# Two Fourier-and-GLU layers on one core: the first quad's row sums as f32 products with scaled diagonals, and a new order for the opening

## The chip, the cores and the metric

The kernel runs on one core of one Trainium2 chip. The core has TensorE (PE) for matmuls, whose results land in the eight banks of PSUM, VectorE (DVE), ScalarE (ACT), GpSimd (POOL) and SyncE (SP), which here issues most DMAs. Each engine works through its own queue in order. The time is that of one execution of the program on the chip, in microseconds; a kernel's figure is the median of its runs.

## The reference

Two rounds of the same two layers on `x` (2048 rows of 640), all in f32:

```python
x = x + _A_ref(_layernorm(x), dft_seq_re, dft_seq_im, dft_hid_re, dft_hid_im)
x = x + _B_ref(_layernorm(x), w_gate, w_up, w_down)
# _A_ref: a = x @ hid_re.T; b = x @ hid_im.T; y = seq_re @ a - seq_im @ b
# _B_ref: h = sigmoid(x @ w_gate) * (x @ w_up); y = h @ w_down     (F = 1728)
```

## The kernel before

**Folding.** The Fourier matrices are symmetric, so the kernel adds and subtracts mirrored rows and columns first and multiplies by a quarter of the matrix. The 2048 rows stand in four *quads* (i = 0 to 3) of four *groups* of 128 rows each, A, B, C and D (GA to GD). Within a row, column c and column 640 - c are added (the even half e, 321 columns) and subtracted (the odd half o, 320 columns): `fold_columns`, in the opening's list `cg i g` for one group and `col i k` for two. The rows of B and C are needed in reverse order: they are loaded as they lie, multiplied by a reversed identity on PE in f32 (`turn`, into a pair of PSUM banks called a twin), and brought back to SBUF by ACT (`turned`).

**Scale and join.** LayerNorm gives every row a factor; the statistics come from `stats`, `square` and `means`, the factor from `power` (ACT) and `scale` (DVE), into `quads[i]`, column 19, and the constants from the means into `coef[i]`. Then `re` and `ro` (ACT, L783 and L785) scale the even and odd halves of B and D, `dd` (DVE, L788; `de` and `do`, L792, for quad 1) adds scaled A and C to them, and `join` (DVE, L829) forms A + C and A - C. So every quad ends as two e parts and two o parts.

**High and low halves.** Everything that PE multiplies in the dense work is f16 in two parts. `jhi` (ACT, L839) rounds to f16, `jlo` (DVE, L845, and a small copy on ACT, L849) writes what is left. `chi` and `clo` do so for the sequence matrix, `whhi` and `whlo` for the hidden one, `wshi` and `wslo` for the gate and up weights (all L269 on ACT and L271 on DVE).

**Products.** `seq i tp` (PE, L980) multiplies quad i by its part of the sequence matrix, tp = 0 for the even and 1 for the odd rows; quads 0 and 1 sum into one set of banks and 2 and 3 into another. `evhi` and `ev` bring these sums out as high and low f16. `hid q ph` (PE, L1065) multiplies by the hidden matrix; `hidev`, `first`, `im`, `sums`, `difs` and `add` bring the result into x. The second LayerNorm of the first rows (`nst`, `cen`, `nvar`, `npow`, `nscale`, `nhi`, `nlo`), transposes (`tp`, `tph`, `tpl`) and the first gate and up products (`gu`, L1343) end the opening. After it the program runs the rest of the two rounds from a planner's list with due times; the change leaves that list alone.

**Order.** The opening's order is written out by hand in one string, `OPENING`. Its steps are emitted one after the other, and each goes to the end of its engine's queue, so the string fixes the order on every engine. `junk n` is n f16 matmuls of zeros (L376) with no reader. The loads of x, of the sequence matrix and of the first weights are issued by SP ahead of all of it (`wld` loads later weights). Before, PSUM is divided in the opening into two twins (two banks each) and four single banks; after the last `turned` the twins' four banks become single ones (`drop_twins`).

SBUF is one tensor, `big`, from which `take` hands out slots; their addresses come from a search over the times at which they are taken and dropped.

Of the kernel before, what the change touches and what calls it, by code (L numbers as in the profile page):

```python
# [138 lines left out]
class Slot:  # L139
# [37 lines left out]
    first 1, first 0, hid 0 1, wslo 0 1, ev 1 1 1, ev 1 1 0, wslo 1 0, evhi 1 1 2, im, sums, hid 1 0, hidev 1 0,  # L177
    hid 1 1, hid 2 0, add 0, nst 0, hidev 1 1, cen 0, wshi 0 0, difs, add 1, hidev 2 0, nst 1, nvar 0, wslo 0 0,
    cen 1, npow 0, nscale 0, ev 1 1 2, nst 2, nst 3, nhi 0, nhi 1, cen 3, nvar 1, nlo 0, nlo 1, npow 1, mid, hid 2 1,
    tp 0, tp 1, tph 0, wld 4 0, wld 3 1, wld 4 1, wld 3 0, tpl 0, tpl 1, nscale 1, tph 1, cen 2, nhi 3, midhi, gu 0 0,  # L180
# [1976 lines left out]
```

## Time and profile before

| | |
|---|---|
| runs | 1142.88, 1141.91, 1138.86 us; median 1141.91 |
| profiled execution | 1141.29 us, of which the span 1139.5 |
| mean granted TensorE clock | 0.994 |
| PE busy | 1110.4 us, 97% of the span, 9030 matmuls |
| DVE, ACT, POOL busy | 761.8, 538.5, 348.8 us |
| first `seq` product, first `hid` product, first `gu` product | 40.20, 67.55, 85.77 us |

In a row of the timeline the start (us) comes first, then the length, the engine, the line of the kernel, the operation, what it writes and reads, the shape, and xN where N instructions were merged; in brackets is the idle time of the engine before it and what ended that. In a row of groups the busy time and the mean of one instruction in ns stand behind the bar. In a row by stretch the busy time of PE, PEld (weight loads), DVE, ACT and POOL follow the length, then the granted clock (1.00 is full), the DMA engines' share and GB/s. In a row of waits stand the total in us, how often, and the longest.

### The profile page before, as it was taken

The page shows a single profiled execution, that of the slowest core. Times are in us where ns is not written, and L with a number is a line of the kernel's source. Part 1 is how long each engine was busy: PE and PEld are TensorE (multiplying, and loading weights), DVE is VectorE, ACT ScalarE, POOL GpSimd, SP SyncE. Part 2 cuts the span into 40 slices and gives each one's busy share as a digit, 9 for nine tenths or more (in the row PEclk, how much of TensorE's full clock was granted, in tenths as well). Part 3 has the DMA queues.
Part 4 walks back from the last instruction along what each step waited for, and adds up shares of the span by engine and source line. Part 5 has one row for each costly group of instructions (what it writes and reads, how often), then busy time and mean ns, then how long its engine had stood idle before and what let it go on. Part 6 is the DMA issues. An engine that isn't in the chain of part 4 may idle for free. (4 is left out here: it accounts for less than half of the span.)

```text
span 1139.5 us, 23456 instructions
## 1 busy us (share of the span) xinstructions
PE 1110.4 (97%) x9030; PEld 883.1 (78%) x9030; DVE 761.8 (67%) x1678; ACT 538.5 (47%) x1187; POOL 348.8 (31%) x568
## 2 busy tenths in 40 slices
PE   5799999999999999999999999999999999999997
PEld 3668446788878887788878888778887888788875
DVE  6994998766656877485667877834674668426751
ACT  6975583355534653255525544314541555225430
POOL 1001564432445353431350203031553322132001
PEclk9989999999999999999999999999999999999999
DMA  8434685877595756968521662474957973799411
GB/s 247 151 125 156 240 312 157 246 244 221 164 238 193 243 181 174 244 212 302 193 108 43 186 222 94 125 240 164 265 168 150 322 238 104 100 238 292 157 41 39
DMA packets 154447, 214.72 MB, mean 188 GB/s; under 512 B 74655, under 2 KB 99505, under 8 KB 154326
## 3 DMA queue, kind: packets, MB, share of 16 engines
q1 hardware_dynamic: 135622, 165.04, 48.7%
q0 software_dynamic: 18560, 47.93, 14.1%
q8 instruction: 72, 1.18, 0.4%
q14 instruction: 49, 0.40, 0.1%
q10 hardware_dynamic: 144, 0.16, 0.0%
HBM read 173.04 MB, written 25.44 MB: 174 GB/s over the span
## 5 line engine op out<-in xcount | busy, mean ns | idle before, releaser
L1390 PE MATMUL acc<-big 128*128 128x256 f16 x4698 | 516.6, 273 | 1.8 <-ACT big L1394 1.4
L1390 PEld LDWEIGHTS <-big 128*128 128x128 f16 x4698 | 459.6, 98 | 56.4 <-issue 1.5
L1547 PE MATMUL acc<-big 128*128 128x320 f16 x2624 | 357.7, 299 | 0.0
L1547 PEld LDWEIGHTS <-big 128*128 128x128 f16 x2624 | 256.7, 98 | 99.5
L1608 POOL DMA_DIRECT2D big<-in_ct x256 | 174.3, 686 | 269.2 <-DVE big L1617 145.2
L1394 ACT ACTIVATE big<-acc 128x256 f32<-128x256 f32 x348 | 130.3, 382 | 233.2 <-PE acc L1390 229.6
L1458 DVE TENSOR_TENSOR big<-big 128x512 f16<-128x512 f32 x87 | 59.9, 689 | 112.3 <-ACT big L1457 112.3
L1580 ACT ACTIVATE big<-big 128x768 f32<-128x768 f32 (+10 forms) x110 | 81.3, 739 | 89.4 <-DVE big L1617 72.7
L1343 PE MATMUL acc<-big 128*128 128x256 f16 (+1 forms) x705 | 114.6, 325 | 0.5 <-ACT big L673 0.5
L1343 PEld LDWEIGHTS <-big 128*128 128x128 f16 x705 | 68.9, 98 | 45.0 <-issue 0.7
L1436 ACT ACTIVATE big<-big 128x512 f32<-128x512 f32 x87 | 53.4, 628 | 53.6 <-DVE big L1427 53.2
L271 DVE SCALAR_TENSOR_TENSOR big<-big 128x640 f16<-128x640 f32 (+7 forms) x82 | 62.9, 799 | 7.3 <-ACT big L269 7.2
L1446 DVE SCALAR_TENSOR_TENSOR big<-acc,big 128x256 f32<-128x256 f32 x87 | 36.4, 419 | 40.2 <-PE acc L1390 34.7
L1562 DVE SCALAR_TENSOR_TENSOR big<-acc,big 128x320 f32<-128x320 f32 x64 | 28.3, 483 | 49.5 <-PE acc L1547 49.5
L617 ACT ACTIVATE big<-big 128x384 f16<-128x384 f32 (+2 forms) x48 | 28.6, 645 | 69.2 <-DVE big L599 49.1
L1427 DVE TENSOR_TENSOR big<-big,acc 128x512 f32<-128x512 f32 x87 | 59.2, 680 | 1.3 <-PE acc L1390 1.1
L269 ACT ACTIVATE big<-big 128x640 f16<-128x640 f32 (+7 forms) x82 | 51.0, 657 | 17.8 <-POOL big L1284 7.1
L1457 ACT ACTIVATE big<-big 128x512 f16<-128x512 f32 x87 | 54.5, 626 | 7.9 <-DVE big L1448 6.5
L1625 POOL DMA_DIRECT2D big<-in_ct x40 | 27.3, 687 | 90.4 <-ACT big L1580 52.5
L438 POOL DMA_INDIRECT out<-big,rows x8 | 9.5, 1182 | 125.5 <-DVE fin L1705 55.1
L1615 DVE TENSOR_TENSOR big<-big 128x256 f32<-128x256 f32 x64 | 26.9, 420 | 26.6 <-DMA big<-in_ct 26.6
L1614 DVE TENSOR_TENSOR big<-big 128x256 f32<-128x256 f32 x64 | 26.5, 415 | 24.1 <-DMA big<-in_ct 23.8
(242 smaller groups left out, 1095.5 us busy)
## 6 DMA issues: line engine op xcount, KB each, us to landing
big<-kept_s SPq DMA_DIRECT2D x84, 512.0 KB, 8.0
big<-kept_w SPq DMA_DIRECT2D x115, 320.0 KB, 4.3
big<-in_ct POOLq DMA_DIRECT2D x256, 128.0 KB, 4.5
big<-kept_w SPq DMA_DIRECT2D x74, 192.0 KB, 6.0
kept_w<-big SPq DMA_DIRECT2D x27, 320.0 KB, 3.7
big<-in_ct POOLq DMA_DIRECT2D x32, 256.0 KB, 5.5
kept_s<-big SPq DMA_DIRECT2D x13, 512.0 KB, 5.2
big<-in_wg SPq DMA_DIRECT2D x18, 320.0 KB, 3.0
```

Of the source, the lines that this page charges most:

```text
L269: nc.scalar.activation(dh, src, AF.Copy, scale=s)
L271: nc.vector.scalar_tensor_tensor(dl, src, s, dh, op0=OP.mult, op1=OP.subtract)
L1343: nc.tensor.matmul(ps, w[wp][:, d * P : (d + 1) * P], xt[:, xp, :], start=(d == 0 and wp == HI and xp == HI), stop=(d == ND - 1 and wp == LO))
L1390: nc.tensor.matmul(ps, wt, xt, start=start and n == 0, stop=n == len(todo) - 1, skip_group_check=not start)
L1394: nc.scalar.activation(dst, ps, AF.Copy)
L1427: nc.vector.tensor_tensor(v, v, other, op=OP.add)
L1436: nc.scalar.activation(v, v, AF.Sigmoid, scale=SG)
L1457: nc.scalar.activation(s.parts[HI], v, AF.Copy)
L1458: nc.vector.tensor_tensor(s.parts[LO], v, s.parts[HI], op=OP.subtract)
L1547: nc.tensor.matmul(held["pd", e][0][:, :EH], held["ht", j].parts[hp][:, i * P : (i + 1) * P], held["w", 2, j].parts[wp][:, e * EH : (e + 1 ...
L1580: nc.scalar.activation(v, v, AF.Square, accum_out=new_sum()[:p])
L1608: nc.gpsimd.dma_start(v[:, g], bass.AP(ct.tensor, (r * S + row) * S, [[P, NS], [d * S, 16], [1, P]]))
```

## The change

For quad 0 alone the four `re` and `ro` steps, the two `dd` steps and `join` are gone. Instead `ident 2` makes a 128x128 f32 identity and its negative (DVE); `dg 0` scales them by the rows' factors, seven diagonals in all (ACT); `ps 0` makes the two e parts and the two o parts as sums of four f32 products each, diagonal times group, in two twins (PE); `mj 0` forms the sum and the difference of the two constants of the means (DVE). `jhi 0` and `jlo 0` read from PSUM; for e they add the constant by the way, one instruction for each of the two parts. PSUM in the opening is now three twins and two single banks, and a step `free` in the list marks where the twins end. (`pj`, `join_products`, is defined and not used.) The list `OPENING` is made anew from end to end, with other places and numbers of fillers. The core of the diff (the rest of the list goes on with the same kinds of steps):

```diff
-    turn 0 B, turned 0 B, cg 0 3, ident 0, cg 0 1, turn 0 C, turned 0 C, turn 1 B, double 0, means 0, turn 1 C,
-    chi 1 0, square 0 B, chi 0 0, junk 6, square 0 C, turned 1 B, stats 0 A, cg 0 0, stats 1 A, clo 1 0, junk 13,
-    turned 1 C, cg 0 2, stats 0 D, clo 0 0, chi 1 1, means 1, square 1 B, power 0, square 1 C, col 1 0, stats 1 D,
-    col 1 1, turn 2 B, scale 0, turned 2 B, stats 2 A, power 1, turn 2 C, turned 2 C, junk 3, junk 11, double 1,
-    re 0 1, double 2, scale 1, chi 1 2, means 2, col 2 1, clo 1 1, row 0, row 1, turn 3 B, whhi 1, junk 5, ro 1 0,
-    ro 1 1, square 2 B, re 1 1, re 1 0, clo 1 2, col 2 0, whlo 1, chi 0 1, ro 0 1, square 2 C, do 1 1, de 1 1, de 1 0,
-    stats 2 D, whhi 2, re 0 0, ro 0 0, dd 0 1, do 1 0, join 1, junk 3, dd 0 0, join 0, whhi 5, chi 0 2, jhi 1 o,
-    power 2, junk 14, whhi 0, scale 2, row 2, junk 10, jhi 0 o, ro 2 0, jhi 0 e, turned 3 B, re 2 0, jhi 1 e, re 2 1,
-    whlo 5, whlo 0, jlo 0 e, jlo 0 o, junk 12, clo 0 1, turn 3 C, junk 5, turned 3 C, col 3 0, junk 3, stats 3 A,
-    seq 0 1, junk 2, junk 12, jlo 1 o, whhi 3, means 3, c512hi, jlo 1 e, row 3, dd 2 0, seq 1 1, stats 3 D, ro 2 1,
-    col 3 1, c512lo, seq 0 0, square 3 B, evhi 0 1 0, evhi 0 1 1, chi 1 3, wshi 0 1, square 3 C, whlo 3, dd 2 1,
-    ev 0 1 0, ev 0 1 1, join 2, chi 0 3, clo 1 3, power 3, double 3, jhi 2 e, evhi 0 1 2, scale 3, re 3 1, jhi 2 o,
-    ro 3 1, seq 1 0, whhi 4, re 3 0, wshi 2 0, ro 3 0, evhi 0 0 0, jlo 2 e, clo 0 2, clo 0 3, jlo 2 o, junk 13,
-    dd 3 1, ev 0 1 2, ident 1, dd 3 0, join 3, ev 0 0 0, whlo 4, evhi 0 0 2, seq 2 1, jhi 3 e, jhi 3 o, wshi 2 1,
-    evhi 0 0 1, wshi 1 1, jlo 3 e, jlo 3 o, seq 2 0, whlo 2, ev 0 0 2, ev 0 0 1, wslo 1 1, seq 3 0, seq 3 1,
-    evhi 1 0 1, evhi 1 1 1, evhi 1 0 0, wshi 1 0, ev 1 0 1, hid 0 0, evhi 1 1 0, evhi 1 0 2, ev 1 0 0, ev 1 0 2,
...
+    turn 0 B, turned 0 B, stats 0 D, cg 0 3, stats 0 A, cg 0 1, ident 0, turn 0 C, junk 13, turned 0 C, means 0,
+    turn 1 C, turn 1 B, chi 0 0, square 0 B, chi 1 0, double 0, square 0 C, turned 1 B, clo 1 0, turned 1 C, junk 13,
+    ident 2, stats 1 A, cg 0 2, means 1, square 1 B, power 0, chi 1 1, col 1 0, junk 13, junk 8, scale 0, clo 0 0,
+    stats 1 D, cg 0 0, col 1 1, turn 2 B, dg 0, square 1 C, mj 0, turned 2 B, power 1, stats 2 A, turn 2 C,
+    turned 2 C, double 1, ps 0, junk 15, double 2, scale 1, junk 10, ro 1 1, chi 1 2, means 2, col 2 1, row 0,
+    col 2 0, row 1, clo 1 1, junk 3, turn 3 B, whhi 1, re 1 0, ro 1 0, square 2 B, square 2 C, re 1 1, clo 1 2,
+    chi 0 1, whlo 1, stats 2 D, whhi 2, jhi 0 o, junk 14, junk 5, de 1 0, de 1 1, do 1 1, do 1 0, join 1, junk 1,
+    whhi 5, chi 0 2, jhi 1 o, power 2, junk 4, whhi 0, scale 2, row 2, turned 3 B, ro 2 0, re 2 0, jhi 0 e, jhi 1 e,
+    re 2 1, whlo 5, jlo 0 o, whlo 0, jlo 1 o, clo 0 1, jlo 0 e, turn 3 C, junk 4, junk 5, turned 3 C, free, col 3 0,
+    stats 3 A, junk 2, seq 0 1, whhi 3, ro 2 1, c512hi, jlo 1 e, row 3, dd 2 0, seq 1 1, stats 3 D, means 3, col 3 1,
+    c512lo, seq 0 0, evhi 0 1 0, wshi 0 1, evhi 0 1 1, whlo 3, dd 2 1, chi 1 3, square 3 C, square 3 B, ev 0 1 0,
+    junk 5, join 2, ev 0 1 1, clo 1 3, power 3, double 3, jhi 2 e, evhi 0 1 2, scale 3, chi 0 3, ro 3 1, seq 1 0,
+    re 3 1, junk 14, jhi 2 o, re 3 0, junk 12, whhi 4, ro 3 0, evhi 0 0 0, clo 0 2, jlo 2 e, clo 0 3, ev 0 1 2,
+    dd 3 1, junk 18, jlo 2 o, junk 14, dd 3 0, join 3, ident 1, whlo 4, ev 0 0 0, evhi 0 0 2, seq 2 1, jhi 3 e,
+    jhi 3 o, wshi 2 0, evhi 0 0 1, wshi 1 1, jlo 3 e, jlo 3 o, seq 2 0, whlo 2, ev 0 0 1, wslo 1 1, ev 0 0 2, seq 3 0,
+    seq 3 1, evhi 1 0 1, wshi 2 1, evhi 1 0 0, evhi 1 1 1, hid 0 0, evhi 1 0 2, ev 1 0 0, ev 1 0 1, ev 1 1 1,
...
-    acc = [psum.tile([P, 512], F32, name=f"acc{i}") for i in range(4)]
+    acc = [psum.tile([P, 512], F32, name=f"acc{i}") for i in range(2)]
...
-    banks = list(range(4))
+    banks = list(range(2))
...
+    eye = [take(1, "eye", k).f32 for k in range(2)]
...
+        elif k == 2:
+            nc.vector.tensor_scalar(eye[0], ramp[:, ::-1], part[:, 33:34], None, op0=OP.is_equal)
+            nc.vector.tensor_scalar(eye[1], ramp[:, ::-1], part[:, 33:34], -1.0, op0=OP.is_equal, op1=OP.mult)
...
-    twins = [twin_pool.tile([P, 2, 512], F32, name=f"twin{k}") for k in range(2)]
+    twins = [twin_pool.tile([P, 2, 512], F32, name=f"twin{k}") for k in range(3)]
...
-        acc.extend(others.tile([P, 512], F32, name=f"acc{i}") for i in range(4, 8))
-        free_bank(4, 5, 6, 7)
+        acc.extend(others.tile([P, 512], F32, name=f"acc{i}") for i in range(2, 8))
+        free_bank(*range(2, 8))
...
+    def scaled_eyes(i):
+        t, v = quads[i], take(7, "diag", i).f32
+        for n, (g, k) in enumerate(SIGNED):
+            nc.scalar.activation(v[:, n * P : n * P + P], eye[k], AF.Copy, scale=t[:, g, 19:20])
+    def means_joined(i):
+        for tp, op in enumerate((OP.add, OP.subtract)):
+            nc.vector.tensor_tensor(quads[i][:, tp : tp + 1, 21], coef[i][:, 0:1], coef[i][:, 1:2], op=op)
+    def scaled_products(i):
+        pair, v = [twins.pop(0) for _ in range(2)], held["diag", i].f32
+        for n, w in enumerate((EC, EH)):
+            at_banks[i, n] = pair[n][:, :, :w], pair[n]
+            for tp in range(2):
+                half = (tp + n) % 2
+                for g, k in ((GA, 0), (GB, n), (GC, half), (GD, (half + n) % 2)):
+                    m = SIGNED.index((g, k))
+                    nc.tensor.matmul(pair[n][:, tp, :w], v[:, m * P : m * P + P], folds(i)[n][:, g], start=g == GA, stop=g == GD)
+        drop("diag", i)
+        with_means.add(i)
+    SIGNED = ((GA, 0), (GB, 0), (GC, 0), (GD, 0), (GB, 1), (GC, 1), (GD, 1))
+    with_means = set()
+    at_banks = {}
...
     def drop_rev():
         for k in range(2):
             drop("rev", k)
+            drop("eye", k)
...
+            if (i, n) in at_banks:
+                src, twin = at_banks[i, n]
+                if 2 in do:
+                    twins.append(twin)
+                    del at_banks[i, n]
+            shift = quads[i][:, :2, 21] if i in with_means and n == 0 and not folding[0] else None
-                nc.scalar.activation(take_parts(key, i)[:, at, 0, :w], src[:, at], AF.Copy)
+                if shift is None:
+                    nc.scalar.activation(take_parts(key, i)[:, at, 0, :w], src[:, at], AF.Copy)
+                else:
+                    for tp in range(2):
+                        nc.scalar.activation(take_parts(key, i)[:, tp, 0, :w], src[:, tp], AF.Identity, bias=shift[:, tp : tp + 1])
-                nc.vector.tensor_tensor(p[:, :, 1, :w], src[:, at], p[:, :, 0, :w], op=OP.subtract)
+                if shift is None:
+                    nc.vector.tensor_tensor(p[:, :, 1, :w], src[:, at], p[:, :, 0, :w], op=OP.subtract)
+                else:
+                    for tp in range(2):
+                        nc.vector.scalar_tensor_tensor(p[:, tp, 1, :w], src[:, tp], shift[:, tp : tp + 1], p[:, tp, 0, :w],
+                                                       op0=OP.add, op1=OP.subtract)
...
-            "turn": turn_round, "turned": turned, "means": turned_means, "square": turned_squares,
+            "turn": turn_round, "pj": join_products, "dg": scaled_eyes, "mj": means_joined, "ps": scaled_products, "turned": turned, "means": turned_means, "square": turned_squares,
...
-            todo[f](*a)
-            if (f, a) == ("turned", [last, GC]):
+            if f != "free":
+                todo[f](*a)
+            if f == "free":
                 drop_rev()
                 drop_twins()
```

More of the change, by code (lines that the diff above doesn't have):

```diff
@@ L176 @@
-    evhi 1 0 1, evhi 1 1 1, evhi 1 0 0, wshi 1 0, ev 1 0 1, hid 0 0, evhi 1 1 0, evhi 1 0 2, ev 1 0 0, ev 1 0 2,
[L177 to L180, printed above, removed]
@@ new lines @@
+    re 3 1, junk 14, jhi 2 o, re 3 0, junk 12, whhi 4, ro 3 0, evhi 0 0 0, clo 0 2, jlo 2 e, clo 0 3, ev 0 1 2,
+    dd 3 1, junk 18, jlo 2 o, junk 14, dd 3 0, join 3, ident 1, whlo 4, ev 0 0 0, evhi 0 0 2, seq 2 1, jhi 3 e,
+    jhi 3 o, wshi 2 0, evhi 0 0 1, wshi 1 1, jlo 3 e, jlo 3 o, seq 2 0, whlo 2, ev 0 0 1, wslo 1 1, ev 0 0 2, seq 3 0,
+    seq 3 1, evhi 1 0 1, wshi 2 1, evhi 1 0 0, evhi 1 1 1, hid 0 0, evhi 1 0 2, ev 1 0 0, ev 1 0 1, ev 1 1 1,
+    evhi 1 1 2, evhi 1 1 0, wslo 0 1, ev 1 0 2, first 1, first 0, wshi 1 0, hid 0 1, ev 1 1 0, wslo 1 0, im, sums,
@@ new lines @@
+    hid 1 0, hidev 1 0, hid 1 1, hid 2 0, add 0, nst 0, hidev 1 1, wshi 0 0, cen 0, difs, add 1, hidev 2 0, nst 1,
+    nvar 0, ev 1 1 2, wslo 0 0, npow 0, nscale 0, nst 2, cen 1, nst 3, nhi 0, nhi 1, nvar 1, nlo 0, wld 4 0, wld 4 1,
+    cen 3, mid, hid 2 1, nlo 1, npow 1, tp 0, tp 1, tph 0, wld 3 1, wld 3 0, tpl 0, tpl 1, nscale 1, tph 1, cen 2,
+    wslo 2 0, nhi 3, nhi 2, midhi, gu 0 0, hidev 2 1, nlo 2, nlo 3, tp 2, tp 3, tpl 2, tph 3, hid 3 0, wshi 3 0,
+    hidev 3 0, hid 3 1, tph 2, wshi 4 1, wshi 3 1, tpl 3, wshi 4 0, hidev 3 1, wslo 3 1, wslo 3 0, gu 1 0, gu 0 1,
@@ L185 @@
+    gu 1 1, wslo 2 1, wslo 4 1, middif, wslo 4 0, gu 2 0, gu 2 1"""
 ON_ACT = {(2, GA), (2, GD), (3, GA), (3, GD)}
@@ L219, in homes_for @@
         big = pool.tile([P, (UNITS + 2 * CK) * UNIT], F32, name="big")
-        acc = [psum.tile([P, 512], F32, name=f"acc{i}") for i in range(4)]
+        acc = [psum.tile([P, 512], F32, name=f"acc{i}") for i in range(2)]
         flag = pool.tile([P, 1], I32, name="flag")
@@ L817, in fold_row, with join_products @@
             drop("row")
+    def join_products(i):
+        pair = [twins.pop(0) for _ in range(2)]
+        for n, w in enumerate((EC, EH)):
+            at_banks[i, n] = pair[n][:, :, :w], pair[n]
+            for tp in range(2):
+                for q, k in ((GA, 0), (GC, (tp + n) % 2)):
+                    nc.tensor.matmul(pair[n][:, tp, :w], eye[k], folds(i)[n][:, q], start=q == GA, stop=q == GC)
+    def scaled_eyes(i):
[7 more added lines that the diff above has]
+        pair, v = [twins.pop(0) for _ in range(2)], held["diag", i].f32
+        for n, w in enumerate((EC, EH)):
+            at_banks[i, n] = pair[n][:, :, :w], pair[n]
+            for tp in range(2):
[8 more added lines that the diff above has]
+    at_banks = {}
     def drop_rev():
```

4 lines of the change are left out of this document (1 added, 3 removed).

## The prediction

> **What bounds the kernel now.** I read the page first, then the waits of TensorE over the whole span, the busy time by stretch, and the timeline of the first 100 us engine by engine.
>
> ```profile
> span 1139.5 us, 23456 instructions
> PE 1110.4 (97%) x9030; PEld 883.1 (78%) x9030; DVE 761.8 (67%) x1678; ACT 538.5 (47%) x1187; POOL 348.8 (31%) x568
> PE twin L400 <- DMA big<-in_x: 13.8, 5, 6.6
> PE acc L980 <- DVE big L845: 2.0, 4, 0.7
> 25.00:57.00 32.00, 22.47 (x167) 17.20 (x167) 30.54 (x58) 31.59 (x75) 1.11 (x6) 0.88 0.49 163
> 80.00:95.00 15.00, 13.95 (x126) 10.28 (x125) 10.31 (x25) 13.01 (x25) 5.89 (x8) 1.00 0.37 134
> 95.00:300.00 205.00, 205.00 (x1492) 145.81 (x1490) 154.14 (x270) 104.68 (x212) 85.15 (x111) 1.00 0.71 227
> ```
>
> TensorE is busy 97% of the span and all of 95 to 300, so the opening can only give what lets that dense part begin earlier. In the rows by stretch, the columns after the length are PE, PEld, DVE, ACT and POOL busy, granted clock, DMA share and GB/s. Between 25 and 57 us ACT is busy 31.59 of 32 us and DVE 30.54, while much of PE's 22.47 is `junk`, matmuls on zeros that only keep the clock up. So two queues, DVE and ACT, pace the opening. The timeline shows what ends last:
>
> ```profile
> 18.69 2.39 PE L400 MATMUL twin<-big 128*128 128x320 f32 x8 [0.86 <-DMA big<-in_x]
> 29.21 2.47 PE L400 MATMUL twin<-big 128*128 128x320 f32 x4 [6.60 <-DMA big<-in_x]
> 36.82 1.24 PE L400 MATMUL twin<-big 128*128 128x320 f32 x4
> L376 PE MATMUL acc<-big 128*128 128x256 f16 x112 | 13.7, 279 | 0.0
> 43.24 1.69 PE L376 MATMUL acc<-big 128*128 128x256 f16 x14
> 57.30 10.41 PE L980 MATMUL acc<-big 128*128 128x256 f16 x67 [0.75 <-DVE big L845]
> 67.55 15.73 PE L1065 MATMUL acc<-big 128*128 128x321 f16 x111
> 62.15 1.55 DVE L845 TENSOR_TENSOR big<-big 128x642 f16<-128x642 f32 x2
> ```
>
> From 57.30 PE hardly stops. Its products of quad 3 cannot run before the last low halves of quad 3, the pair at L845, which ends at 62.15 + 1.55 = 63.7. Fillers and products of this size start 0.109 us apart (14 fillers take 1.69 us, the last of them its 0.279: 1.41/13). So the 36 products of quad 3 then end at 67.6, and 67.55 is where the hidden-direction products (L1065) start. So DVE's queue up to `jlo 3 o` sets the opening, and what it loses counts one for one, unless ACT holds it up.
>
> **ACT: what goes and comes.**
>
> ```profile
> L783 ACT ACTIVATE big<-big,coef,quad 128x321 f32<-128x321 f32 x8 | 5.1, 643 | 0.2 <-DVE coef L772 0.2
> L785 ACT ACTIVATE big<-big,quad 128x320 f32<-128x320 f32 x8 | 4.3, 546 | 0.0
> L269 ACT ACTIVATE big<-big 128x640 f16<-128x640 f32 x2 | 1.4, 721 | 0.0
> L269 ACT ACTIVATE big<-big 128x321 f16<-128x321 f32 x2 | 0.9, 458 | 0.0
> L411 ACT ACTIVATE quad<-quad 128x2 f32<-128x2 f32 x4 | 0.8, 191 | 0.0
> 29.20 1.19 ACT L783 ACTIVATE big<-big,coef,quad 128x321 f32<-128x321 f32 x2
> 76.74 0.75 ACT L1114 ACTIVATE big<-acc 128x321 f32<-128x321 f32 x2
> 39.41 0.73 ACT L839 ACTIVATE big<-big 128x642 f16<-128x642 f32 x1
> ```
>
> Two L783 in a row take 1.19, not 1.29: the next starts 0.1 before the last ends, so an operation occupies its duration less 0.1. The two `re 0` and two `ro 0` go: 2 x 0.55 + 2 x 0.45 = 2.0 us. `dg 0` adds seven 128x128 scalings by a column. Nearest are 128x2 (191 ns) and 128x320 with such a column (546 ns), so seven occupy between 0.7 and 3.1 us. The two L269 rows give (721 - 458)/319 = 0.82 ns per column, so 128 columns cost 546 - 192 x 0.82 = 0.39, occupying 0.29: seven are 2.05 us. `jhi 0 e` becomes two biased evictions from PSUM: between 0.75 (two L1114, no bias) and 1.19 (two L783), I take 0.92, against 0.63 occupied by one L839. `jhi 0 o` costs what it did. ACT's sum: -2.0 + 2.05 + 0.3 = +0.35 us.
>
> **DVE: what goes and comes.**
>
> ```profile
> L788 DVE SCALAR_TENSOR_TENSOR big<-big,quad 128x641 f32<-128x641 f32 x6 | 5.3, 882 | 0.4 <-ACT big L785 0.3
> 36.19 1.56 DVE L829 TENSOR_TENSOR big<-big 128x641 f32<-128x641 f32 x2
> 37.67 0.16 DVE L430 SCALAR_TENSOR_TENSOR quad<-quad 128x4 f32<-128x4 f32 x1
> 8.33 0.28 DVE L356 TENSOR_SCALAR big<-big 128x128 f32<-128x128 f32 x1
> 2.94 0.58 DVE L342 TENSOR_SCALAR big<-big 128x128 f32<-128x128 f32 x1
> 72.48 0.88 DVE L1133 SCALAR_TENSOR_TENSOR big<-acc,big 128x321 f32<-128x321 f32 x2
> 40.17 1.56 DVE L845 TENSOR_TENSOR big<-big 128x642 f16<-128x642 f32 x2 [0.43 <-ACT big L839]
> L772 DVE TENSOR_TENSOR coef<-quad 128x2 f32<-128x2 f32 x4 | 0.6, 160 | 0.0
> ```
>
> Two `dd 0` (0.8 occupied each) and `join 0` (36.19 to 37.67, 1.5) go: 3.1 us. `ident 2` adds two 128x128 compares, between 0.28 (L356) and 0.58 (L342) each; L356 is the same compare, so 0.5 us together, at about 13 us where the queue waits for x anyway. `mj 0` adds two tiny sums, 0.25. `jlo 0 e` becomes two operations from PSUM, 0.88 like the L1133 pair, against 0.78, half of the L845 pair: +0.1. DVE's sum is -3.1 + 0.5 + 0.25 + 0.1 = -2.25.
>
> **PE.** `ps 0` is 16 f32 products. Each `turn` is two f32 products and shows as four records: 2.47 at half clock (29.21), 1.24 at full (36.82). So `ps 0` is 32 records of 0.31 = 9.9 us, or 19.8 at half clock. It needs `dg 0`, and that needs `power 0`:
>
> ```profile
> 17.05 0.19 ACT L411 ACTIVATE quad<-quad 128x2 f32<-128x2 f32 x1
> 18.10 0.29 ACT L425 ACTIVATE quad<-quad,eps 128x4 f32<-128x4 f32 x1
> 20.05 0.70 ACT L406 ACTIVATE big<-twin 128x640 f32<-128x640 f32 x1 [0.85 <-PE twin L400]
> 21.86 0.74 ACT L718 ACTIVATE big<-big 128x640 f32<-128x640 f32 x1 [1.02 <-DMA big<-in_x]
> 36.71 0.29 ACT L425 ACTIVATE quad<-quad,eps 128x4 f32<-128x4 f32 x1
> 21.67 0.16 DVE L430 SCALAR_TENSOR_TENSOR quad<-quad 128x4 f32<-128x4 f32 x1
> ```
>
> Before, `power 0` ends at 18.4, but `scale 0` starts only at 21.67, behind other work. In the new order it follows at once, so the seven diagonals run from 18.5 to 20.6, in the time that ACT spends on the two waits of 0.85 and 1.02. On DVE `clo 0 0`, `stats 1 D` and `cg 0 0` come between, some 2.5 us, so the last operand is there at about 21.4; `turn 2 C` ends at 21.1 as now. `ps 0` then runs from 21.4 to 31.3, where PE waited 6.60 us for x before. That wait is its cover. `turn 3 B` and the fillers move behind it, to about 35, ahead of `turned 3 B` at 38.
>
> **The two queues together.** ACT from `means 1` (17.05) to `power 2` (36.71) took 19.66 us, 1.87 of them waits, so 17.8 of work. New: 17.8 - 2.0 + 2.05 + 0.6 (`jhi 0 o`, now ahead of it) + 0.57 (`chi 1 1`, now behind `means 1`) = 19.0. `means 1` starts near 16.6, because turn 1 C and 1 B now end at 15.1 and are evicted after it, and 0.2 of waits remain, so `power 2` comes at 35.8 and `jhi 0 o` at about 33.4, 2 us after `ps 0`. Behind `jhi 0 o` on ACT are queued `whhi 5`, `chi 0 2`, `jhi 1 o` and `power 2`, and DVE's `scale 2` waits for the last. DVE, rid of `dd 0` and `join 0`, is ready for `scale 2` at about 34.0 and stands until 36.1, where it came at 37.67 before: 1.6 us gained, the rest of the 2.25 lost to that wait. From there to `jlo 3 o` DVE has the same list, 26.0 us long, 0.43 less by the wait at L845 that goes and 0.1 more by `jlo 0 e`: end at 61.8, 1.9 earlier. The products of quad 3 follow, L1065 starts near 65.7, and the chain of first rows behind it moves along. In 80 to 95 PE idles 1.05 us; the moved steps there (`cen 1`, `nhi 2`, `nlo 2`) may return 0.1 of it. No DMA is added; the four `wld` loads on SP only change places among themselves, with nothing queued between. Sum: -2.0 us.
>
> The profiled execution took 1141.29, its span of 1139.5 and 1.8 around it; the median of the runs is 1141.91. So 1139.3 for such an execution, 1139.9 as a median.
>
> **The clock.** Fillers at half rate would cost twice, and the clock's rows bear on it:
>
> ```profile
> 20.92 1.69 PE L376 MATMUL acc<-big 128*128 128x256 f16 x14
> 25.00:30.00 5.00, 0.79 (x2) 0.62 (x3) 4.93 (x10) 4.93 (x14) 0.31 (x1) 0.57 0.86 269
> 55.00:60.00 5.00, 3.29 (x17) 2.22 (x17) 4.96 (x9) 4.64 (x10) 0.00 (x0) 0.65 0.61 177
> ```
>
> PE stood from 22.6 to 29.21 and the granted clock in 25 to 30 was 0.57; it thinned out after 51 and got 0.65 in 55 to 60. The new order has no such hole: 34 fillers run into turn 2 B, and 58 (14, 12, 18 and 14) stand ahead of `seq 2 1`. The Trainium skill (TensorE: Matmul & The Clock Gate, "What's actually happening") says that an idle window of about 3.4 us halves the clock, that a busy one restores it, and that the window runs free of the kernel's start. The trace's 6.6 us hole agrees. By that rule `ps 0` is 9.9 us, as summed, but the fillers' phase may differ between runs.
>
> **The rivals.**
> *The clock's share adds on (0.13).* The 57.30 row holds 69 products, some at half clock: 10.41 us instead of 69 x 0.109 = 7.5. If PE and not `jlo 3 o` bounded that part, the steady clock would give up to 2.7 more: 1137.2. Against it: the 63.7 of DVE fits 67.55 to 0.1.
> *ACT eats it (0.17).* At 3.1 us for the seven diagonals and 1.19 for the biased pair ACT is 1.3 later, and with DVE's list bound to it the gain falls to 0.7 or, with the slots laid out anew, to nothing: 1141.2 to 1141.9.
> *The fillers become work (0.15): slower.* The 58 fillers take 6.3 us. From `seq 0 1`, due at 41.0 (DVE's list from `scale 2` to `jlo 0 e` is 4.9 long), 80 matmuls of 0.109 and 0.4 of short waits bring PE to them at 50.1; it leaves at 56.4, just as `jlo 2 o` is ready; `seq 2` needs 3.9 us ahead of 61.8, so the slack is 1.5. If `seq 0 1` is over 1.5 late, every further us goes to the end. At half clock the fillers take 12.6 and cost 6.3 - 1.5 = 4.8, for a net of +2.8: 1144.7. Were `ps 0` itself at half clock, it would end at 41, `jhi 0 o` would stand 7.8 us and the net be +5.8: 1147.7. For it: in-order fillers wait for nobody. Against it: PE is dense from 12 us on.
>
> **How the numbers follow.** The forecast has 0.55. Its own range runs from all of DVE's 2.25 plus the cheap diagonals (-3.5) to the dear ones (-0.7): 1138.4 to 1141.2. The runs of before lie 3.1 below to 1.0 above their median, so the 8-in-10 range goes down to 1136.5 and, into the rival with the fillers, up to 1144.5. 0.5% is 5.7 us, about what a measurement here can tell from no change: faster than 1136.2 takes the clock's share and luck, 0.1; slower than 1147.6 takes half clock on `ps 0` or a layout of slots that stalls the dense part, 0.1; 0.8 is left between.
>
> **What would show it.** Right: 32 f32 records at 0.31 from about 21.4 to 31.3; `scale 2` near 36; the last L845-like pair of quad 3 ending near 61.8; L1065 near 65.7; granted clock 1.00 from 16 to 95. Wrong: f32 records at 0.6, ACT standing at `jhi 0 o`, PE going from fillers into `seq 2 1` after 58 without a wait, or new waits of PE after 95.

## The result and the profile after

The kernel after takes 1136.42 us (median of 21 runs, 1135.54 to 1140.23); the kernel before, run beside it, 1138.61 (21 runs, 1137.52 to 1142.88). The two medians differ by 2.2 us. The ratio over the runs is 0.9976, 95% interval 0.9968 to 0.9984, which is 2.7 us, inside the 0.5% that the chances called no change. The forecast of 1139.9 was 3.5 too high, and the time lies 0.08 below the range of 1136.5 to 1144.5.

The page of the kernel after, its waits of TensorE, and its busy time by stretch:

```profile
span 1134.5 us, 23654 instructions
PE 1118.4 (99%) x9123; PEld 892.3 (79%) x9123; DVE 757.5 (67%) x1679; ACT 539.5 (48%) x1191; POOL 347.7 (31%) x568
PE twin L404 <- DMA big<-in_x: 4.7, 3, 3.7
PE acc L1445 <- DMA big<-big: 1.1, 1, 1.1
25.00:57.00 32.00, 30.73 (x242) 25.11 (x241) 29.53 (x56) 31.12 (x73) 1.65 (x8) 1.00 0.60 194
```

TensorE's wait for x is down from 13.8 to 4.7 us, and between 25 and 57 it is busy 30.73 of 32 us at full clock instead of 22.47 at 0.88; the products of `ps 0` and fillers make up the difference. ACT is as full as before there. The timeline of the opening, PE and then ACT and DVE:

```profile
11.71 2.39 PE L404 MATMUL twin<-big 128*128 128x320 f32 x8 [1.03 <-DVE big L358]
20.55 8.79 PE L850 MATMUL twin<-big 128*128 128x321 f32 x32
49.01 6.50 PE L380 MATMUL acc<-big 128*128 128x256 f16 x58
59.07 5.03 PE L1035 MATMUL acc<-big 128*128 128x256 f16 x42 [0.28 <-DVE big L271]
63.94 15.55 PE L1120 MATMUL acc<-big 128*128 128x321 f16 x111
14.83 0.70 ACT L410 ACTIVATE big<-twin 128x640 f32<-128x640 f32 x1
16.71 0.29 ACT L429 ACTIVATE quad<-quad,eps 128x4 f32<-128x4 f32 x1
17.64 2.16 ACT L835 ACTIVATE big<-big,quad 128x128 f32<-128x128 f32 x7
21.19 0.29 ACT L429 ACTIVATE quad<-quad,eps 128x4 f32<-128x4 f32 x1
21.38 0.73 ACT L722 ACTIVATE big<-big 128x640 f32<-128x640 f32 x1
34.64 0.29 ACT L429 ACTIVATE quad<-quad,eps 128x4 f32<-128x4 f32 x1
34.96 0.17 DVE L434 SCALAR_TENSOR_TENSOR quad<-quad 128x4 f32<-128x4 f32 x1 [1.84 <-ACT quad L429]
58.93 1.55 DVE L896 TENSOR_TENSOR big<-big 128x642 f16<-128x642 f32 x2
```

The three L429 rows are `power 0`, `power 1` and `power 2`, L404 the `turn`s, L410 the second `turned` of quad 1, L835 `dg 0`, L850 `ps 0`, L434 `scale 2`, L896 the last `jlo`, L1120 `hid`. All the steps that the change names are there. `hid` starts at 63.94, where it started at 67.55.

In the kernel before, `power 1` stands on ACT behind `stats 2 A`, which waits for quad 2's x (the row at 21.86 in the prediction). In the kernel after the two have changed places (the rows at 21.19 and 21.38 above). These are the second `turned` of quad 1 and `power 1` in the kernel before:

```profile
15.79 0.70 ACT L406 ACTIVATE big<-twin 128x640 f32<-128x640 f32 x1 [1.22 <-PE twin L400]
23.55 0.29 ACT L425 ACTIVATE quad<-quad,eps 128x4 f32<-128x4 f32 x1
```

So two marks carry what follows: the start of `power 1`, and the time from there to the first `hid` product. All times in us, from the one trace of each kernel; the medians are of 4 to 21 runs, and the kernel before was run beside each group (1138.61 to 1139.22).

| kernel | `power 1` | to `hid` | `hid` | median | ratio to before (95%) |
|---|---|---|---|---|---|
| before | 23.55 | 44.00 | 67.55 | 1138.61 | |
| e1_before_again | 22.96 | 43.88 | 66.84 | 1139.43 | 1.0001 (0.9989 to 1.0012) |
| after | 21.19 | 42.75 | 63.94 | 1136.42 | 0.9976 (0.9968 to 0.9984) |
| e14_after_again | 21.76 | 43.17 | 64.93 | 1136.34 | 0.9976 (0.9965 to 0.9987) |
| e2_order_only | 21.91 | 45.30 | 67.21 | 1137.44 | 0.9981 (0.9970 to 0.9992) |
| e3_method_only | 22.48 | 44.50 | 66.98 | 1140.63 | 1.0015 (1.0003 to 1.0026) |
| e4_before_clock | 22.08 | 43.60 | 65.68 | 1138.07 | 0.9991 (0.9982 to 1.0000) |
| e5_before_x2 | 21.23 | 43.50 | 64.73 | 1136.89 | 0.9980 (0.9958 to 1.0002) |
| e6_after_x2 | 21.25 | 42.67 | 63.92 | 1136.73 | 0.9968 (0.9950 to 0.9987) |
| e7_order_late | 21.80 | 44.04 | 65.84 | 1137.50 | 0.9976 (0.9958 to 0.9994) |
| e8_better | 22.38 | 47.60 | 69.98 | 1174.51 | 1.0299 (1.0276 to 1.0322) |
| e9_dg_twice | 23.85 | 44.09 | 67.94 | 1140.09 | 1.0009 (0.9994 to 1.0023) |
| e10_fill_more | 21.20 | 46.66 | 67.86 | 1140.13 | 1.0007 (0.9996 to 1.0019) |
| e11_fill_none | 21.98 | 42.89 | 64.87 | 1135.93 | 0.9970 (0.9959 to 0.9981) |
| e12_power2_early | 22.08 | 42.75 | 64.83 | 1139.15 | 1.0005 (0.9989 to 1.0020) |
| e13_dg_split | 21.01 | 44.49 | 65.50 | 1136.00 | 0.9976 (0.9965 to 0.9986) |

Over two traces of each kernel, `hid` moves from a mean of 67.2 to 64.4, 2.8 us; the two groups' medians differ by 2.2 and 2.6, the ratios give 2.7. The gain is in the opening: 1.8 of it in front of `power 1`, 1.0 behind. The 1.8 have two parts. ACT starts the second `turned` of quad 1 at 15.79 and 15.38 in the kernel before, at 14.83 and 15.39 in the kernel after, 0.5 earlier in the mean; from there to `power 1` it takes 7.76 and 7.58 before, 6.36 and 6.37 after, 1.3 less. The waits for quad 2's x stood in this second part.

### The profile page after: what moved, and what is told of

Same layout as the page of the kernel before. It is cut to its first block, busy times and chain, and to the rows that moved or that the text cites. A ratio compares the mean times of both kernels' runs of the same rounds, so it can differ in the third digit from the quotient of the medians.

```text
span 1134.5 us, 23654 instructions
## 1 busy us (share of the span) xinstructions
PE 1118.4 (99%) x9123; PEld 892.3 (79%) x9123; DVE 757.5 (67%) x1679; ACT 539.5 (48%) x1191; POOL 347.7 (31%) x568
## 5 line engine op out<-in xcount | busy, mean ns | idle before, releaser
L1481 DVE TENSOR_TENSOR big<-big 128x256 f32<-128x256 f32 x87 | 36.4, 418 | 7.7 <-ACT big L1449 7.6
L1669 DVE TENSOR_TENSOR big<-big 128x256 f32<-128x256 f32 x64 | 26.5, 415 | 21.5 <-DMA big<-in_ct 21.5
```

## The experiments

**The kernel before once more, and with the clock kept full.** e1_before_again is the kernel before unchanged. e4_before_clock has 24 fillers more, so that TensorE does not thin out after 51 us:

```diff
-    ... clo 0 2, clo 0 3, jlo 2 o, junk 13,
+    ... clo 0 2, clo 0 3, jlo 2 o, junk 37,
```

> The kernel before, unchanged, to see how much one execution of it differs from another: the profiled execution of before took 1141.29 us, the median of its runs is 1138.61. Theory Q (the queues of DVE and ACT set the opening): the first hidden product (L1065) starts within 0.5 us of 67.55 again, and where the time is nearer to 1138.6 the missing 2 to 3 us lie behind 95 us, in the dense part. Theory C (the half clock of 56.5 to 63.3 us sets it, and it falls differently in each execution): L1065 starts at 64.5 to 66 in an execution whose granted clock is full there, and the time follows. Ratio to before 1.000 by both.

> The kernel before with 37 fillers instead of 13 ahead of seq 2 1, which fill PE's holes of 53.3 to 57.3 us so that the clock stays full; nothing else is changed. Theory Q: quad 3's low halves on DVE still end at 63.7, hidden products start at 67.3 to 67.6, ratio 1.000. Theory C: the products of quads 2 and 3 run at full clock, hidden products start 2 to 2.7 us earlier, at 64.9 to 65.5, ratio 0.9976 to 0.998.

```profile
57.00:80.00 23.00, 21.16 (x160) 14.95 (x159) 20.78 (x40) 16.72 (x36) 1.80 (x2) 1.00 0.26 74
```

With the clock at 1.00 from 57 to 80, the time from `power 1` to `hid` is 43.60 instead of 44.00 and 43.88, the ratio 0.9991. So the half clock on the kernel before's last `seq` products was worth 0.4 us at most, not the 2.7 of the rival "the clock's share adds on". `hid` itself came at 65.68 mainly because `power 1` came at 22.08: that mark moves by 1.5 us over three traces of the same old order.

**The order alone.** e2_order_only takes the new list with `re`, `ro`, `dd` and `join` of quad 0 kept, `ident 2` and `mj 0` left out, and 80 fillers in the place of `ps 0`; e7_order_late differs in where `dd` and `join` stand:

```diff
-    dg 0, square 1 C, mj 0, ... ps 0, junk 15, double 2, scale 1, ...
+    re 0 1, ro 0 1, re 0 0, ro 0 0, square 1 C, ... junk 80, junk 15, double 2, scale 1, dd 0 1, dd 0 0, join 0, ...
# e7: dd 0 1, dd 0 0, join 0 behind join 1, jhi 0 o behind row 2
```

> The new order, three twins and fillers, but quad 0 scaled and joined the old way: re 0 and ro 0 (four, 2.0 us of ACT) stand at the place of dg 0, dd 0 and join 0 (3.1 us of DVE) behind scale 1, and 80 fillers (8.7 us) at the place of the products. Theory Q: DVE pays 3.1 us more, of which its 1.84 us wait at scale 2 hides most, and jlo 0 e and mj 0 save 0.5, so it loses 0.8 to 1.3 of the 3.6 us by which L1120 came earlier (63.94 against 67.55): hidden products start at 64.7 to 65.3, ratio to before 0.9983 to 0.9987. If the gain were the method's own, they would start at 67 or later, ratio 1.000. If it were the clock's alone, at 64, ratio 0.9976.

> The new order with quad 0 scaled and joined the old way, as in the run that put dd 0 and join 0 behind scale 1, but with dd 0 1, dd 0 0 and join 0 (3.1 us of DVE) behind join 1, where DVE stands 1.84 us for power 2 in the kernel after, and jhi 0 o later. Theory Q: DVE comes to scale 2 at 36.2 instead of 34.96, hidden products start at 65.0 to 65.5, ratio to before 0.9983 to 0.9988: the order alone is worth 1.7 to 2.2 us of the 3.0 to 3.6, the method the rest. If order alone is worth nothing: 67, ratio 1.000; if all: 64, 0.9976.

Both have `power 1` at 21.8 to 21.9, as early as the kernel after, but need 45.30 and 44.04 from there. So the earlier `power 1` belongs to the order. Behind it the kernel after is 1.3 us shorter than the better of the two (44.04 to 42.75), and 0.9 by its second trace (43.17). That is where the products can save, but not all of it need be theirs: TensorE ran at half clock in e7 from 42 to 44, where the kernel after had 1.00. The run times don't separate the two: e7's ratio, 0.9976, is the kernel after's own. Nor do e2's times follow its trace: 1137.44 with `hid` no earlier than before. Its part behind the opening was 1041.7 us from the second stretch of `gu` products to the end, before's 1044.5 and 1045.9.

**The method alone.** e3_method_only puts `dg 0, ps 0` into the old list where `re 0 1` stood, without the steps that they replace and without 44 fillers:

```diff
-    ... scale 0, turned 2 B, ... double 1, re 0 1, double 2, scale 1, ...
+    ... scale 0, mj 0, turned 2 B, ... double 1, dg 0, ps 0, double 2, scale 1, ...
```

> The old order with the products: dg 0 and ps 0 stand where re 0 1 stood, mj 0 behind scale 0, ident 2 behind ident 0, and the 44 fillers between turn 3 B and turn 3 C are left out, since the products take PE's time. Theory Q: DVE is rid of 3.1 us and gets 0.8, but ACT, which has nothing taken off it (+0.35) and whose waits ahead of 22 us stay, sets power 2 as before, so hidden products start 0 to 1.5 us earlier than 67.55; ratio 0.9987 to 1.000. Products start near 26.6, after a hole of 4 us on PE, and may run at half clock (19.8 us, until 46): then jhi 0 stands on ACT and the ratio is 1.004 to 1.008. If the method were the gain: 64.5, ratio 0.9976.

No gain: 44.50 from `power 1`, the ratio 1.0015 (1.0003 to 1.0026). The timeline shows what went otherwise, first on PE, then on DVE:

```profile
23.88 8.90 PE L850 MATMUL twin<-big 128*128 128x321 f32 x32 [1.21 <-ACT big L835]
32.62 1.24 PE L404 MATMUL twin<-big 128*128 128x320 f32 x4
39.90 2.50 PE L404 MATMUL twin<-big 128*128 128x320 f32 x4 [6.05 <-ACT big L410]
25.71 0.83 DVE L734 TENSOR_TENSOR big<-big 128x640 f32<-128x640 f32 x1 [1.49 <-ACT big L748]
39.20 1.01 DVE L899 SCALAR_TENSOR_TENSOR big<-twin,quad,big 128x321 f16<-128x321 f32 x2 [1.24 <-ACT big L889]
```

`ps 0` starts 3.3 us later than in the kernel after. `turned 3 B` still stands late in the old list, `turn 3 C` waits 6.05 us for its twin, and then runs at half clock; the 44 fillers that this run lacks would have stood in that hole, so the half clock is in part its own doing. DVE, rid of 3.1 us, waits for ACT instead: 1.49 and 1.24 us in the rows above and 1.32 at `scale 2`, where the kernel before's longest waits from `power 1` to `hid` are 1.17, 0.43 and 0.34. So the method in the old order gains nothing. The new order without it gains in e7 1.4 of the 2.8 us at `hid` (65.84 against the mean of 67.2), in e2 nothing there, and in the run times of both about as much as the whole change.

**Quad 2's x.** SP issues the loads of x in order. Ahead of quad 2's stand three small loads (`load_c512`) that wait until POOL has cleared their slot: in the trace of before

```profile
SPq L928 <- POOL big L926: 1.4, 1, 1.4
14.94 0.81 SPq L928 DMA_DIRECT2D big<-in_ct  x3
15.80 1.77 SPq L390 DMA_DIRECT2D big<-in_x  x4
```

e5_before_x2 and e6_after_x2 move these three behind quad 2's, in the kernel before and after, and nothing else:

```diff
+            if i == 2:
+                load_c512()
             for r in range(2):
                 load_c(r, i)
-            if i == 1:
-                load_c512()
```

> The kernel before with one move: the three small loads of the 512th row of the sequence matrix (c512), which wait on SP for a memset on POOL (14.39 to 14.91) and hold the loads of quad 2 behind them until 15.80, are issued behind these loads. So quad 2's rows are issued near 12.7 and land 2 to 3 us earlier. Theory A (the wait of ACT for quad 2's group A, 1.02 us, and of PE for its group B, 0.85, are on before's path, and the new order gains by filling them): hidden products start 1.0 to 1.6 us earlier, at 65.3 to 66.3, ratio 0.9986 to 0.999. If these waits are hidden anyway: 66.8 to 67.5, ratio 1.000.

> The same move of the c512 loads in the kernel after, where ACT does not wait for quad 2's group A any more and PE waits 0.5 us for its group B. Theory A: hidden products start 0 to 0.4 us earlier than 63.94, ratio to before 0.9972 to 0.9976. If arrival still bounds it: 62.5 to 63, ratio 0.9965.

```profile
16.23 0.68 ACT L269 ACTIVATE big<-big 128x514 f16<-128x514 f32 x1 [0.76 <-DMA big<-in_ct]
19.55 0.73 ACT L718 ACTIVATE big<-big 128x640 f32<-128x640 f32 x1
21.23 0.29 ACT L425 ACTIVATE quad<-quad,eps 128x4 f32<-128x4 f32 x1
```

These are e5's rows. In the kernel before with this move, quad 2's loads go out at 12.66 instead of 15.80, and ACT no longer stands in front of `stats 2 A` (19.55). `power 1` is 1.7 and 2.3 us earlier than in the two traces of before, `hid` (64.73) 2.1 and 2.8. From `chi 1 1` on (16.23, where ACT waits for the sequence matrix) it takes 5.00 to `power 1`, before 7.07 and 6.28, and 6.04 in e4, whose list is the same up to there: the move is worth 1.0 to 2.1. The median is 1136.89, but with six runs the interval of the ratio reaches 1.0002, so the run times alone don't show the gain. In the kernel after the same move changes nothing (21.25 and 63.92). So this one move in the old order comes near the new one at `power 1` (21.23 against 21.19 and 21.76), and the larger part of what the new order gains there, 1.3 of 1.8 us, lies in the stretch where that wait stood.

**What paces the new opening.** e9_dg_twice makes each diagonal twice (2.2 us of ACT were expected), e10_fill_more puts 40 more fillers ahead of `seq 2 1`, e11_fill_none takes all 58 away:

```diff
# e9
-        for n, (g, k) in enumerate(SIGNED):
+        for n, (g, k) in [x for x in enumerate(SIGNED) for _ in range(2)]:
# e10: junk 18 -> junk 58 behind dd 3 1;  e11: junk 14, junk 12, junk 18, junk 14 out
```

> The kernel after with each of the seven scaled diagonals made twice: seven more ScalarE instructions of 0.31 us, 2.2 us, in front of power 1; the numbers computed are the same. Theory P (the diagonals stand on the path that sets the opening: ScalarE is the engine that ends last in the first 50 us): power 2 moves from 34.6 to 36 to 37 us, the first hidden product from 63.94 to 65.5 to 66.2, the time is 1.5 to 2.2 us above the kernel after's. Theory Q (the twin products and VectorE set it, and ScalarE's waits at jhi 0 o and scale 2 take it up): the first hidden product at 63.9 to 64.8, the time within 0.8.

> The kernel after with 40 more filler matmuls (18 to 58, about 4.5 us of TensorE by 6.50 us for 58) in front of seq 2 1. Theory P (the prediction's: TensorE has a slack of about 1.5 us there, and what goes beyond it becomes work on the path): the first hidden product at 66.5 to 68.4 instead of 63.94, the time 2.5 to 4.5 us longer. Theory Q (the hidden product waits for VectorE's joins and not for TensorE, so that fillers lie beside them): at 63.9 to 65, time within 1.

> The kernel after without the 58 filler matmuls in front of seq 2 1 (6.50 us of TensorE). Theory P (they are cover alone: the granted clock falls below 1.00 in the windows after 50 us, and the first dense products are slowed): the first hidden product at 63.9 to 65, the first gu product 1 to 2.7 us later than 82.17, the time 0.5 to 2.7 us longer. Theory Q (TensorE is full enough without them, the clock stays at 0.97 or more): every mark within 0.4 us, the time within 0.5. Theory R (they stand in the way of the last steps): the first hidden product 0.5 to 1.5 us earlier and the time shorter by as much.

```profile
17.26 5.19 ACT L835 ACTIVATE big<-big,quad 128x128 f32<-128x128 f32 x14
```

e9: fourteen diagonals took 5.19 us, 3.03 more than seven and not 2.2. From `means 1` to `power 1` ACT takes 8.58 us instead of 5.54, so all of it goes on; `means 1` itself was 0.4 earlier here. `power 1` is 2.7 later than in the kernel after, `power 2` 2.6, and `hid` 4.0, more than either theory had. The rest is clock: TensorE stood 2.91 us at `turn 3 C`, and came back at half of it. The same two rows in the kernel after and in e9:

```profile
37.10 1.34 PE L404 MATMUL twin<-big 128*128 128x320 f32 x4 [1.00 <-ACT big L410]
38.28 1.36 PE L380 MATMUL acc<-big 128*128 128x256 f16 x11
```

```profile
39.68 2.50 PE L404 MATMUL twin<-big 128*128 128x320 f32 x4 [2.91 <-ACT big L410]
41.98 2.55 PE L380 MATMUL acc<-big 128*128 128x256 f16 x11
53.73 6.50 PE L380 MATMUL acc<-big 128*128 128x256 f16 x58
60.06 8.04 PE L1035 MATMUL acc<-big 128*128 128x256 f16 x72
67.94 2.35 PE L1120 MATMUL acc<-big 128*128 128x321 f16 x16
```

From there TensorE runs without a gap into `hid`: late by 1.16 and 1.19 us in these two rows, it had become the bound, and the 58 fillers were work. So the rivals "ACT eats it" and "the fillers become work" both describe real prices; they did not fall due, because the seven diagonals took 2.16 us and not 3.1, and the clock held.

```profile
49.29 10.86 PE L380 MATMUL acc<-big 128*128 128x256 f16 x98
```

e10: 98 fillers take 10.86 us, 4.36 more, and the time from `power 1` to `hid` grows by 3.91 (42.75 to 46.66), the median by 3.7. The slack was 0.45 us, or 0.87 against the kernel after's second trace (43.17), and not the 1.5 of the prediction.

e11: without any filler the granted clock falls to 0.50 between 54 and 58 us, and `hid` still comes 42.89 behind `power 1`, against 42.75 and 43.17; the median is 1135.93. Here the expectation that the time would be 0.5 to 2.7 longer failed. The waits of TensorE for the high and low halves, with fillers gone (1.90 us for ACT's L886, 1.13 for DVE's L896), show that DVE and ACT set the mark, and that the slow products fit between. They fit narrowly: e13, below, also has no fillers, and its last products ran at half clock for longer (the rows of e11, then of e13; those by stretch as above):

```profile
54.00:56.00 2.00, 0.61 (x2) 0.13 (x2) 2.00 (x3) 2.00 (x5) 0.00 (x0) 0.50 1.07 335
56.16 8.88 PE L1035 MATMUL acc<-big 128*128 128x256 f16 x67 [1.13 <-DVE big L896]
58.00:60.00 2.00, 2.00 (x16) 1.59 (x14) 2.00 (x5) 1.41 (x3) 0.00 (x0) 0.75 0.00 0
```

```profile
55.81 9.85 PE L1038 MATMUL acc<-big 128*128 128x256 f16 x67 [1.15 <-DVE big L899]
58.00:60.00 2.00, 2.00 (x11) 1.41 (x10) 2.00 (x6) 1.76 (x3) 0.00 (x0) 0.50 0.00 0
```

The same 67 products took 0.97 more, and the last of them bound `hid`. So in the traces the 58 fillers buy between nothing and 1 us, by when the clock returns; the medians (1135.93 and 1136.00 without, 1136.42 and 1136.34 with) show no gain from them.

**DVE's wait at `scale 2`.** The prediction saw DVE stand there for about 2 us; 1.84 it was. e8_better and e12_power2_early move `power 2` right behind `stats 2 D`, with less ACT work ahead of the last joins; e8 also reorders `col 3 0` and `jlo 1 e`, e12 takes e6's order of loads:

```diff
-    chi 0 1, whlo 1, stats 2 D, whhi 2, jhi 0 o, ... jhi 1 o, power 2, junk 4, whhi 0, scale 2, row 2, ...
+    chi 0 1, whlo 1, stats 2 D, power 2, whhi 2, jhi 0 o, ... jhi 1 o, junk 4, whhi 0, scale 2, ...
```

> The kernel after with power 2 moved up on ACT to right behind stats 2 D (four steps, 2.2 us, earlier), so that DVE need not stand 1.84 us at scale 2; col 3 0 ahead of jlo 0 e, jlo 1 e behind it; whhi 4, evhi 0 1 2 and chi 0 3 behind ro 3 0 on ACT, clo 0 3 and ev 0 1 2 behind join 3 on DVE; 17 fillers fewer ahead of seq 2 1. Theory Q: the wait was on the path, hidden products start 1.0 to 1.8 us earlier, at 62.1 to 62.9, ratio to before 0.996 to 0.9967. If ACT paces everything from there on: 63.5 to 64.0, ratio 0.9973 to 0.9976.

> The kernel after with power 2 right behind stats 2 D instead of behind five other ScalarE steps, jhi 0 e and jhi 1 e in front of row 2, 17 fillers fewer, four ScalarE steps of the half sums moved behind ro 3 0 and join 3, and quad 2's x asked for ahead of the c512 loads. Theory P (VectorE's wait of 1.84 us for power 2 at scale 2 stands on the path): scale 2 starts at 33 to 34 us instead of 34.96, the first hidden product at 62 to 63.3 instead of 63.94, the time 0.5 to 2 us below the kernel after's. Theory Q (ScalarE's sum of work paces the opening; the wait only moves): the first hidden product at 63.5 to 64.5, the time within 0.6.

e8 came out 3% slower, and not for that reason. Its slots got other addresses: by the program's own rule of search, the list as reordered finds no layout with the wider spacing of reuse (8) and takes the narrow one (1); all other kernels here have the wide one. ACT then stands 4.77 us at `double 2`, waiting for nothing that the trace names, and the part behind the opening grows by 29 us:

```profile
29.88 0.21 ACT L748 ACTIVATE big<-big 128x4 f32<-128x4 f32 x1 [4.77 <-issue]
```

That the layout is the cause is argued from the code and not shown by a run of its own.

e12 has the wide spacing and answers the question. `power 2` and `scale 2` come earlier, DVE's wait is gone, and `hid` comes 42.75 behind `power 1`, as in the kernel after to the hundredth:

```profile
33.09 0.30 ACT L429 ACTIVATE quad<-quad,eps 128x4 f32<-128x4 f32 x1
33.84 0.16 DVE L434 SCALAR_TENSOR_TENSOR quad<-quad 128x4 f32<-128x4 f32 x1
51.26 0.17 DVE L434 SCALAR_TENSOR_TENSOR quad<-quad 128x4 f32<-128x4 f32 x1 [0.51 <-ACT quad L429]
PE acc L1445 <- DMA big<-kept_w: 1.4, 1, 1.4
PE acc L1445 <- DMA big<-big: 0.8, 1, 0.8
```

The third row is `scale 3`: DVE now waits for ACT there, where it did not in the kernel after, and 0.30 and 0.50 us at two other places. The wait had only been ACT's total seen from the other side. The last two rows stand for what remains open: 2.2 us of waits for weight loads behind 95 us, and a median 2.7 above the kernel after's, with an opening as long.

**Taking work off ACT, and the kernel after once more.** e13_dg_split makes three of the seven diagonals on DVE and leaves out the fillers as e11 did; e14_after_again is the kernel after unchanged:

```diff
-            nc.scalar.activation(v[:, n * P : n * P + P], eye[k], AF.Copy, scale=t[:, g, 19:20])
+            if n < 4: nc.scalar.activation(...)   # as before
+            else: nc.vector.tensor_scalar(v[:, n * P : n * P + P], eye[k], t[:, g, 19:20], None, op0=OP.mult)
```

> The kernel after without the 58 filler matmuls in front of seq 2 1, and with three of the seven scaled diagonals made by VectorE instead of ScalarE: ScalarE loses 3 x 0.31 = 0.9 us in front of power 1, VectorE gains 3 x 0.28 = 0.8 us. Counted from turn 1's start, since that start varies from one execution to the next by up to 1 us. Theory P (ScalarE's sum of work paces the opening from square 0 B to power 3, and the diagonals on it are a price): power 2 comes 21.9 to 22.4 us behind turn 1's start (the kernel after 22.93, without fillers 22.84), the first hidden product 51.4 to 51.9 us behind it (after 52.23, without fillers 52.38). Theory Q (VectorE is no less full: its 0.8 us eats the gain): power 2 early as in P, but the first hidden product at 52.1 to 53 behind turn 1. The time is within 1.2 us of the kernel after's in either.

> The kernel after itself, a second trace. Theory P (its opening does not hang on when quad 2's x comes in): from turn 1's start to the first hidden product 52.0 to 52.5 us again (52.23 in the first trace), the first hidden product at 63.6 to 65, whatever the part behind 95 us does (1041 to 1046 us, as it did over the executions traced so far). Theory Q (the first trace was a lucky one): more than 53 from turn 1 to the first hidden product, as 55.8 in the kernel before.

e13: ACT is 0.9 us quicker through the diagonals, and loses it at once:

```profile
17.62 1.28 ACT L836 ACTIVATE big<-big,quad 128x128 f32<-128x128 f32 x4
20.32 0.70 ACT L410 ACTIVATE big<-twin 128x640 f32<-128x640 f32 x1 [0.61 <-PE twin L404]
21.78 0.74 ACT L722 ACTIVATE big<-big 128x640 f32<-128x640 f32 x1 [0.47 <-DMA big<-in_x]
```

It waits 0.61 for `turn 2 B` and 0.47 for quad 2's x. `power 2` comes 23.31 behind turn 1's start (34.97 - 11.66), in the kernel after 22.93, and `hid` 53.84: neither theory's numbers. So up to `power 2` ACT is the bound of the new opening by a hair: add to it and everything moves (e9), take from it and the arrival of x is next. e14: from turn 1's start (12.27) to `hid` 52.66, where 52.0 to 52.5 was expected and 52.23 measured first; the whole of the difference lies behind `power 1`, where ACT waits 0.38 for a load of the hidden matrix, as it did not in the first trace:

```profile
27.25 0.57 ACT L269 ACTIVATE big<-big,hs 128x321 f16<-128x321 f32 x1 [0.38 <-DMA big<-in_wh]
```

It is nowhere near the 56.28 and 55.58 of the kernel before.

## Why the prediction came out as it did

**The starting level failed.** The forecast was 1141.91 less 2.0, and the first of these two terms is the step that failed. It was the median of three runs; 11 to 35 runs of the same kernel give 1138.61 to 1139.43. The same sum from 1138.61 is 1136.6, 0.2 from the measured 1136.42. The profiled execution hid this: at 1141.29 it agreed with the three. Its excess lay in the part behind the opening, which the prediction took as fixed: from the second stretch of `gu` products to the end it took 1044.5 us (1045.9 in e1), where the same old order took 1042.6 in e4, and the kernel after 1043.3 and 1042.8. The prediction saw that the runs lay up to 3.1 below their median. It took that off the forecast (1139.9 less 3.1 is 1136.8, the range ended at 1136.5) and not off the lower end of the range for the change itself (1138.4, which would give 1135.3).

**The sum was a little small,** -2.0 against -2.2 by the medians, -2.7 by the ratio and -2.8 at `hid`. What it lacked is turn 1's end (1.0 us at `means 1` in the first trace, 0.4 in e14's) and 0.4 behind `jlo 3 o`. By its steps:

- *`dg 0`* 2.05 us, from 18.5 to 20.6: 2.16, from 17.64. The interpolated 0.29 per diagonal was right; the bounds of 0.7 and 3.1 were far.
- *`ps 0`* 32 records in 9.9 us, 21.4 to 31.3: 32 in 8.79, 20.55 to 29.3. A record of 320 columns inside a long row takes 0.27; the 0.31 came from a row of four with its end.
- *Turn 1* was to end at 15.1, and ended at 14.1: the main miss of the path. The prediction does not show how it came to 15.1; from the start in the kernel before (11.27) that is 3.8 us, near the 4.49 of the slow row there. In all traces of the new list, where 13 fillers stand ahead of it, turn 1 took 2.4.
- *`power 2`* at 35.8, `scale 2` behind a wait of 2: 34.64 and 1.84 (35.63 in e14). The step was right. From `means 1` to `power 2` the prediction had 19.2, with both waits for quad 2's x taken out; it was 18.99 and 19.42. So these waits were in its sum, but as waits that the diagonals would fill; that `power 1` had changed places with `stats 2 A` it did not say.
- *The path.* The prediction put DVE's list on it, unless ACT held it up. ACT does: 3.0 us more of its work move `power 2` and all that follows (e9), and DVE's 1.84 us at `scale 2` can go without moving `hid` (e12).
- *From `scale 2` to the end of `jlo 3 o`* 25.7: 25.5. From there to `hid` 3.9: 3.46.
- *Biased pair* 0.92: 0.94. *`jhi 0 o`* at 33.4 without a stall: 32.52, 3.2 behind `ps 0`. Clock 1.00 from 16 to 95: 1.00.
- *The slack of 1.5 us* under the fillers: 0.45 to 0.87 by e10. The 58 fillers end at 55.5 in the kernel after, and `seq 2 1` follows without a wait.

**The rivals.** "The clock's share adds on" is refuted at its 2.7: it was 0.4 us at most by e4, about the 0.4 by which `hid` came sooner behind `jlo 3 o` than the sum had it. "ACT eats it" and "the fillers become work" are refuted for this change and shown as prices by e9 and e10: 3.0 us of ACT cost 2.7 at `power 1`, 4.4 us of fillers cost 3.9.

**Open.** The part behind the opening moves by up to 4 us from one kernel and one execution to another (1041.7 in e2, 1045.9 in e1). TensorE's waits there explain about half: apart from 0.8 us that all these have in common, 1.8 us in the kernel before, 2.3 in e1 and 2.2 in e12, 1.1 in the kernel after, 0.3 in e4, none in e2. Without them the six parts would still lie between 1041.7 and 1043.6. e2's and e12's medians, 2 to 3 us off from where their openings put them, belong there. No run here settles what sets these waits, nor the rest.

## What to carry to other kernels

Take the level from many runs: a median of three was 3.3 us off here, more than the change was worth. In a queue served in order, look for the step that waits for a load and stands in front of a step that needs none of it; turning the two round, or asking for the load earlier, was worth 1 to 2 us at `power 1` here, no less than a whole new method. A wait on an engine that is full elsewhere is not a gain to be had: DVE's 1.84 us at `scale 2` went without moving the mark.

## What the runs showed of the hardware

After a gap of 2.91 us on TensorE in e9 (36.77 to 39.68) the granted clock was 0.50 from 40 to 44 and 1.00 again from 46; after one of 2.78 in e12 it stayed at 1.00, and the same `turn 3 C` took 1.34 us instead of 2.50:

```profile
39.51 1.34 PE L404 MATMUL twin<-big 128*128 128x320 f32 x4 [2.78 <-ACT big L410]
```

The Trainium skill (TensorE: Matmul & The Clock Gate, "What's actually happening") puts half rate behind at least one idle window of about 3.4 us; in e9 a gap shorter than that was enough, in e12 one nearly as long was not, and no run here shows why. f32 products of 320 columns ran at 0.27 us a record, two records a product, in one row of 32 without a break. A scaling of a 128x128 f32 tile by a column took 0.31 us on ACT (seven in 2.16; 0.37 in e9, where each was written twice, fourteen in 5.19) and 0.22 on DVE in e13:

```profile
21.97 0.67 DVE L838 TENSOR_SCALAR big<-big,quad 128x128 f32<-128x128 f32 x3
```
